# Tile-wise waits between pools, and another order of loads at the head of a channel loop, in a kernel for attention and state-space gradients

## The chip, the core and the metric

The kernel runs on one core of a Trainium2 chip. The metric is the time of one execution on the device in microseconds (us), as a median over runs. Engines are named as in the profile: PE (matmuls), PEld (its weight loads), DVE (VectorE), ACT (ScalarE), POOL (GpSimd) and SP (SyncE, here only a queue that issues DMAs).

## What is computed

The reference is the forward value and the gradients, with respect to twelve inputs, of a gate between two branches:

```python
g = sigmoid((x * gate_w).sum(-1))
a = attention(x, wqkv, wo)                       # S=2048, D=576, 32 heads of 18
b = ssm_conv(x, A, B, C, log_dt, Dskip)          # 576 channels, 128 complex states each
out = g * a + (1 - g) * b
grads = vjp(out)(grad_out)                       # x, wqkv, wo, A, B, C (re, im), log_dt, Dskip, gate_w
```

The convolution's kernel is a sum over states of powers of a complex number per channel; the program computes it by blocks of 128 positions, with a scan over the 16 blocks that carries the state.

## The kernel before

The program is written in four stages, one after the other, each with its own memory pools, opened at its start and closed at its end.

*First stage* (lines 116 to 335). Loads x, the weights and grad_out, transposes, projects Q, K and V, which it stores to QKV_d in DRAM, computes grad_out times wo transposed (dO, lines 245 to 266: ten matmuls for each half of a tile, an evacuation by VectorE or ScalarE, a store to dO_d on SP's queue) and the parameters of the states (lines 268 to 335, stores to par_d). The order on each engine is found by the framework's scheduler, from its own model of time.

*Attention* (lines 429 to 827). Forward and backward in one software pipeline of 1024 steps plus a tail: a step G makes two score products and an exp for the forward pass (PT, line 799) and, OFF = 39 steps later, the backward products, an exp (eb, line 804) and two elementwise products on VectorE (ds, line 809). PT tiles are kept from the one to the other in a pool of 41 buffers of 2 KB per partition (ptp). In the last 39 of the steps with backward work no PT is made. Blocks of ds are transposed by DMA, some by PE (turn, lines 553 to 565), and VectorE copies the transposed ones from PSUM. Meanwhile POOL builds the table of powers E_d for the next stage (lines 343 to 427). The order on all engines, SP included, is that of the source (manual_schedule, line 436). The last work is the gradient stores dqkv_d, issued by POOL (line 537).

*Channel loop* (lines 828 to 1183). The 576 channels are taken in 18 blocks of 32. For each block the program loads windows of x and of the weighted gradient (m_load: xs, gyp), two halves of E (load_en: E1n), parameters (load_par) and, for each pair of blocks, RXn (load_rx); m_part makes correlations (psM), copied to mst by ScalarE and stored to Md_d; m_skw reads them back skewed from DRAM, m_sum and m_fin reduce them into two columns of RX; prep_rx makes the other columns of RX (three ScalarE instructions on RXn); turn_e transposes E with PE and copies it from PSUM; uv projects RX on E (UV); scan runs along the 15 block steps on VectorE (lines 984 to 999: one copy, line 989, then three operations a step); casts, rw1, rw2, t0, ybp, pairs1, pairs2 and sums turn that into outputs and gradient sums; k0 and t0_load take the convolution's first taps through Kp_d in DRAM to T0w. The order on PE, ScalarE, VectorE and POOL is that of the source (line 873); SP's queue is ordered by the scheduler. The lead-in, lines 1112 to 1133, prepares block 0 and part of block 1; the loop then runs from i = -1, where each pass works on block i and prepares i+1, i+2 and i+3. Three pools hold its tiles in SBUF: s4c (results), s4l (constants and gyp) and s4lw (all else).

*Last stage* (lines 1185 to 1393). Loads x, grad_out, the gradient of Q, K and V (dq_all, in four pieces) and others, computes the gradient of wqkv (ps_dwq, line 1257), finishes the states' gradients on VectorE (pool pf), stores them through transposes (emit_dn), closes that pool and opens another in its place (pbwork, line 1329) for the loop over the 16 tiles of tokens (ps_a, ps_dx), which transposes dq_all by DMA (dqT, line 1348).

A pool that opens on the bytes of closed pools waits, all its tiles together, until every user of those pools is done.

Of the kernel before, what the change touches and what calls it, by code (L numbers as in the profile page):

```python
# [17 lines left out]
P = 128  # L18


def build(tc, aps, dbg_aps=None, stages=("s1", "attn", "post", "s4", "final")):
# [40 lines left out]
    with ExitStack() as gctx:  # L62
# [366 lines left out]
        if "attn" in stages:  # L429
# [4 lines left out]
            NFILL = {"V": 1, "Q": 0, "K": 0}  # L434
            with ExitStack() as ctx:
                ctx.enter_context(tc.manual_schedule(engines={mybir.EngineType.PE, mybir.EngineType.Activation, mybir.EngineType.DVE, mybir.EngineType.Pool, mybir.EngineType.SP}))
                ga = ctx.enter_context(tc.tile_pool(name="ga", bufs=2))
                ptp = ctx.enter_context(tc.tile_pool(name="ptp", bufs=41))
                work = ctx.enter_context(tc.tile_pool(name="awork", bufs=2))
                apsp = ctx.enter_context(tc.tile_pool(name="aps", bufs=1, space=bass.MemoryType.PSUM))  # L440
                ident_f = work.tile([P, P], F32, tag="ident_f", bufs=1, name="ident_f")
                nc.vector.tensor_copy(ident_f, ident_bf)

# [109 lines left out]
                def turn(tiles, outs):  # L553

                    pt_ = apsp.tile([P, len(tiles), TPQ, P], BF, tag="accB", name="turn_p")
                    for x, t_ in enumerate(tiles):
                        for qb in range(TPQ):
                            nc.tensor.transpose(pt_[:, x, qb, :], t_[:, qb * P:(qb + 1) * P], ident_bf)  # L558

                    def ev():  # L560
                        x = 0
                        for n, o_ in outs:
                            nc.vector.tensor_copy(o_(), pt_[:, x:x + n])  # L563
                            x += n
                    return ev

# [261 lines left out]
        if "s4" in stages:  # L828
            XB = 2 * CB
            GS = 16  # L830

            s4c_cm = tc.tile_pool(name="s4c", bufs=1)
            s4c = s4c_cm.__enter__()
            SS = s4c.tile([P, 6, D], F32, name="SS")
            CK = s4c.tile([P, 2, 2, D], BF, name="CK")
# [2 lines left out]
            nc.vector.memset(ones_f, 1.0)  # L838

            with ExitStack() as ctx:  # L840
                pc = ctx.enter_context(tc.tile_pool(name="s4l", bufs=1))
                pw = ctx.enter_context(tc.tile_pool(name="s4lw", bufs=1))
                pps = ctx.enter_context(tc.tile_pool(name="s4lps", bufs=1, space=bass.MemoryType.PSUM))
                pidx_i = pc.tile([P, 1], mybir.dt.int32, name="pidx_i")
                nc.gpsimd.iota(pidx_i, pattern=[[0, 1]], base=0, channel_multiplier=1)
                l0col = pc.tile([P, 1], F32, name="l0col")
# [8 lines left out]
                                        base=SUB - 1, pattern=[[SUB, NSUB]], channel_multiplier=-1)  # L855
                gyp2 = []
                for u in range(2):
                    g_u = pc.tile([P, 2 * SUB, CB], BF, name=f"gyp{u}")
                    nc.vector.memset(g_u[:, SUB:2 * SUB, :], 0.0)
                    gyp2.append(g_u)  # L860
                mst2 = []
# [14 lines left out]
                RXs, BK = {}, {}  # L876
                ydx = {}

                def load_rx(xb):
                    d0 = xb * XB  # L880
                    RXn = pw.tile([P, 2 * NB, XB], BF, tag="RXn", bufs=1, name="RXn")
                    nc.sync.dma_start(RXn[:, 0:NB, :], xr_d[:, :, d0:d0 + XB])
                    nc.sync.dma_start(RXn[:, NB:2 * NB, :], gyr_d[:, :, d0:d0 + XB])
                    RXs[xb] = [RXn, None]

                def prep_rx(xb):
# [5 lines left out]

                xss = {}

                def m_load(b):
                    xs = xss[b] = pw.tile([P, NSUB, SUB, CB], BF, tag="xs", bufs=2, name="xs")
                    src = bass.AP(tensor=xb_d.tensor, offset=xb_d[b:b + 1, 0:1, 0:1].offset,
                                  ap=[[XR * SUB * CB, NB], [SUB * CB, NSUB], [1, NSUB * SUB * CB]])
                    nc.sync.dma_start(xs.rearrange("p e t c -> p (e t c)"), src)
                    nc.sync.dma_start(gyp2[b % 2][:, 0:SUB, :].rearrange("p t c -> p (t c)"), gyb_d[b])  # L900

                def m_part(b, u):
                    d0 = b * CB
# [39 lines left out]
                        B_ = BK[b] = dict(E={}, En={})  # L943
                    return BK[b]

                def turn_e(b, h, q0, q1):

                    B_ = blk(b)
                    if q0 == 0:
                        B_["E"][h] = pw.tile([P, GS, 2, N], BF, tag="E1e", bufs=2, name="E1e")  # L950
                    En, E_ = B_["En"][h], B_["E"][h]
                    for q in range(q0, q1):
                        pt_ = pps.tile([P, 4, 2, N], BF, tag="bk", bufs=4, name="etp")
                        for c_ in range(4):
                            for ri in range(2):
                                nc.tensor.transpose(pt_[:, c_, ri, :], En[:, 4 * q + c_, ri, :], ident_bf)  # L956
                        nc.scalar.copy(E_[:, 4 * q:4 * q + 4], pt_)  # L957

                def load_par(b):
                    par = blk(b)["par"] = pw.tile([P, 12, CB], F32, tag="par", bufs=2, name="par")  # L960
                    nc.sync.dma_start(par, par_d[:, 0:12, b * CB:(b + 1) * CB])

                def load_en(b, h):
                    dG = b * CB + h * GS
                    En = blk(b)["En"][h] = pw.tile([P, GS, 2, P], BF, tag="E1n", bufs=6, name="E1n")
                    nc.sync.dma_start(En, E_d[:, dG:dG + GS])

                def uv(b, h):
                    B_ = blk(b)
# [139 lines left out]
                    src = bass.AP(tensor=Kp_d.tensor, offset=Kp_d[b:b + 1, 1:2, 0:1].offset, ap=[[CB, P], [1, P * CB]])  # L1109
                    nc.sync.dma_start(T0w.rearrange("p j c -> p (j c)"), src)  # L1110

                m_load(0)
                load_rx(0)
                load_en(0, 0)
                load_par(0)
                load_en(0, 1)
                m_load(1)
                m_part(0, 0)
                m_part(0, 1)
                m_skw(0)  # L1120
                turn_e(0, 0, 0, 2)
                prep_rx(0)
                turn_e(0, 0, 2, 4)
                m_sum(0)
                m_fin(0)
                k0(0)
                t0_load(0)
                load_en(1, 0)
                load_en(1, 1)
                load_en(2, 0)  # L1130
                load_en(2, 1)
                m_part(1, 0)
                m_part(1, 1)
                for i in range(-1, NBLK):
                    cur = i >= 0
                    nx = i + 1 < NBLK
                    mb = i + 3 if i + 3 < NBLK else None
                    sb = i + 2 if i + 2 < NBLK else None
                    if sb is not None:
                        m_skw(sb)  # L1140
                    if sb is not None:
                        load_par(sb)
                    if mb is not None:
                        m_load(mb)
                    if sb is not None and sb % 2 == 0:
                        load_rx(sb // 2)
                    if nx and cur:
                        k0(i + 1)
                    if nx:
                        uv(i + 1, 0)  # L1150
                        turn_e(i + 1, 1, 0, 4)
                    if sb is not None and sb % 2 == 0:
                        prep_rx(sb // 2)
                    if cur:
                        scan(i, 0, 15)
                        casts(i)
                        rw1(i)
                        rw2(i)
                        t0(i, 0)
                        t0(i, 1)  # L1160
                    if nx:
                        uv(i + 1, 1)
                    if cur:
                        if nx:
                            t0_load(i + 1)
                        ybp(i, 0)
                        ybp(i, 1)
                        pairs1(i)
                    if cur and mb is not None:
                        load_en(mb, 0)  # L1170
                        load_en(mb, 1)
                    if sb is not None:
                        turn_e(sb, 0, 0, 4)
                        m_sum(sb)
                        m_fin(sb)
                    if cur:
                        pairs2(i)
                        sums(i)
                    if mb is not None:
                        m_part(mb, 0)  # L1180
                        m_part(mb, 1)
                    if cur:
                        BK.pop(i)

        if "final" in stages and "s4" in stages:
# [12 lines left out]
                eng.tensor_tensor(out, a, b, op=op)  # L1198

            with ExitStack() as ctx:  # L1200
                pb = ctx.enter_context(tc.tile_pool(name="pb", bufs=1))
                pps = ctx.enter_context(tc.tile_pool(name="pps", bufs=2, space=bass.MemoryType.PSUM))
                pbw = ctx.enter_context(tc.tile_pool(name="pbw", bufs=2))
                x_tok = pb.tile([P, NT, D], BF, name="x_tok_b")
                nc.sync.dma_start(x_tok, x_v)
                dq_all = pb.tile([P, NT, FPAD], BF, name="dq_all")
# [9 lines left out]
                tt(ggo, g_t, omg_t, A.mult)  # L1216

                with ExitStack() as actx:
                    pf = actx.enter_context(tc.tile_pool(name="pf", bufs=1))
                    pfw = actx.enter_context(tc.tile_pool(name="pfw", bufs=2))  # L1220

                    def load_dq(u):
                        f0, fn, c0 = FQS[u]
# [102 lines left out]
                    nc.vector.tensor_copy(rowb2, dDs_row)  # L1326
                    nc.gpsimd.dma_start(aps_out["out_11"].rearrange("(o d) -> o d", o=1), rowb2)

                work = ctx.enter_context(tc.tile_pool(name="pbwork", bufs=2))
                sgo = pb.tile([P, NT], F32, name="sgo")  # L1330
                dsg = pb.tile([P, NT], F32, name="dsg")
                dsgb = pb.tile([P, NT], BF, name="dsgb")
# [107 lines left out]
```

## Time and profile before

| | |
|---|---|
| median of 3 runs | 2973.82 us (2972.2 to 2982.99) |
| the profiled execution | 2978.26 us, its span 2976.5 us |
| busy in the span | PE 2468.2 us (83%), ACT 2373.2 (80%), DVE 2359.4 (79%), POOL 1605.9 (54%) |
| mean granted TensorE clock | 0.917 |
| first exp of attention | 206.13 us |
| last exp of attention, end | 2179.22 us |
| last attention matmul on PE, end | 2187.06 us |
| first scan of the channel loop | 2239.15 us |
| first ps_dwq matmul of the last stage | 2782.41 us |
| first dqT matmul of the token loop | 2869.47 us |

Times of single instructions are microseconds from the span's start. In a timeline a row holds start, duration, engine, line, operation, output and inputs with sizes, count, and in brackets how long the engine had been idle and what ended that. SPq and ACTq are DMA issues on the queues of SP and ScalarE: their duration is the time in which the issuing engine was held, not that of the transfer. The chain of waits is followed back from the last instruction; a row "DMA a<-b" in it is the wait from the issue of a transfer until its data has landed.

### The profile page before, as it was taken

What the parts mean: (1) busy time and instruction counts of PE and PEld (TensorE: products, weight loads), DVE (VectorE), ACT (ScalarE), POOL (GpSimd) and SP (SyncE); (2) the same over time, 40 slices, a digit from 0 to 9 for tenths busy, and PEclk for the clock granted to TensorE, in tenths of its full rate; (3) what the DMA queues carried; (4) which work ended last, traced back from release to release, by engine and by line L of the source; (5) the groups of instructions that cost most, each with busy time, mean ns of one, the idle gap of its engine ahead of it and who ended that gap; (6) DMA issues with size and microseconds to landing.
All of it is one profiled execution on the core that took longest, in us unless ns stands there. A gap on an engine that the chain in (4) does not pass through costs nothing.

```text
span 2976.5 us, 69573 instructions
## 1 busy us (share of the span) xinstructions
PE 2468.2 (83%) x27132; PEld 1186.9 (40%) x27132; DVE 2359.4 (79%) x4147; ACT 2373.2 (80%) x2765; POOL 1605.9 (54%) x2653
## 2 busy tenths in 40 slices
PE   4768988998988888889898889898847887876779
PEld 2432333332333233233333233333226777776457
DVE  4435998997998889799899889989937888889634
ACT  2449999999999999899999999999736777675111
POOL 1038888888887788778888878878010000000010
PEclk8877999998999999899999999999968888887889
DMA  8855999989989989998988998998788877872886
GB/s 224 160 152 107 159 155 169 163 158 165 171 147 165 167 155 167 160 157 155 168 165 154 164 161 153 166 165 153 130 196 217 209 201 208 206 194 66 244 211 132
DMA packets 1293343, 499.99 MB, mean 168 GB/s; under 512 B 1187774, under 2 KB 1263136, under 8 KB 1283796
## 3 DMA queue, kind: packets, MB, share of 16 engines
q1 hardware_dynamic: 1264500, 434.91, 77.2%
q0 software_dynamic: 20624, 53.26, 7.3%
q10 hardware_dynamic: 7888, 7.38, 0.8%
q8 instruction: 212, 3.47, 0.5%
q14 instruction: 119, 0.97, 0.1%
HBM read 144.48 MB, written 99.69 MB: 82 GB/s over the span
## 4 chain that ended last, share of the span: by engine, by line
ACT 34%; DVE 23%; PE 21%; DMA 8%; issue 7%; POOL 4%; SPq 3%; ACTq 0%; DVEq 0%; POOLq 0%
ACT eb L804 20%; ACT PT L799 13%; PE ps_P L30 7%; DVE ds L809 7%; DVE tz L995 3%; DVE HG L999 2%; DVE tz L998 2%; PE accV L30 2%; DMA gT<-gb 2%; PE turn_p L558 2%; PE ps_dx L30 2%; DVE pq L1065 2%; PE ps_dwq L30 1%; POOL et L358 1%; PE accK L30 1%
## 5 line engine op out<-in xcount | busy, mean ns | idle before, releaser
L809 DVE TENSOR_TENSOR ds<-ps_P,PT 128x512 bf16<-128x512 f32 x2048 | 1312.0, 683 | 123.0 <-PE ps_P L30 83.8
L804 ACT ACTIVATE eb<-ps_P 128x1024 bf16<-128x1024 f32 x1024 | 1098.6, 1073 | 71.9 <-PE ps_P L30 70.7
L799 ACT ACTIVATE PT<-ps_P 128x1024 bf16<-128x1024 f32 x1024 | 1101.8, 1078 | 3.7 <-PE ps_P L30 2.5
L30 PE MATMUL ps_P<-dOaT,VaT_g 32*128 32x512 bf16 x2048 | 581.4, 390 | 32.8 <-DVE ds L809 18.3
L358 POOL TENSOR_TENSOR et<-eG,eT 128x448 f32<-128x448 f32 x576 | 542.0, 961 | 10.7
L30 PE MATMUL ps_P<-QaT_g,KaT_g 32*128 32x512 bf16 x2048 | 416.3, 398 | 143.9 <-ACT PT L799 128.5
L30 PE MATMUL ps_P<-KaT_g,QaT_g 32*128 32x512 bf16 x2048 | 408.5, 391 | 2.2 <-ACT eb L804 1.6
L30 PEld LDWEIGHTS <-KaT_g 32*128 32x128 bf16 x2048 | 148.2, 92 | 477.4 <-issue 462.0
L358 POOL TENSOR_TENSOR Eo<-et,et 128x448 bf16<-128x448 f32 x288 | 327.0, 1135 | 20.8
L1101 POOL TENSOR_TENSOR SS<-m 128x96 f32<-128x96 f32 x18 | 7.9, 441 | 556.9 <-ACT m L1099 556.9
L30 PEld LDWEIGHTS <-QaT_g 32*128 32x128 bf16 x2048 | 116.1, 91 | 286.4 <-issue 264.7
L30 PE MATMUL accO<-PT,Vtok_g 128*32 128x512 bf16 x2048 | 214.4, 405 | 0.0
L30 PE MATMUL accV<-eb,dOa 128*32 128x512 bf16 x2048 | 185.3, 395 | 27.6 <-ACT eb L804 27.4
L30 PE MATMUL accK<-dsT,Qtok_g 128*32 128x256 bf16 x4096 | 166.2, 285 | 4.5 <-DMA dsT<-ds 2.8
L558 PE MATMUL turn_p<-ident_bf,ds 128*128 128x128 bf16 x1664 | 137.3, 227 | 29.9 <-DVE gb L630 28.8
L30 PE MATMUL accQ<-ds,Ktok_g 128*32 128x512 bf16 x2048 | 159.2, 388 | 3.2 <-DVE gb L612 2.6
L957 ACT COPY E1e<-etp 128x1024 bf16<-128x1024 bf16 x144 | 135.9, 1044 | 20.0 <-PE etp L956 14.6
L563 DVE COPY dsT<-turn_p 128x1024 bf16<-128x1024 bf16 (+1 forms) x224 | 144.2, 644 | 4.9 <-PE turn_p L558 4.9
L30 PEld LDWEIGHTS <-Vtok_g 128*32 128x32 bf16 x2048 | 53.8, 93 | 225.4 <-issue 224.6
L30 PE MATMUL yp<-Rw,E1n 128*128 128x30 bf16 x1152 | 67.8, 232 | 83.5 <-DVE Rw L1020 69.0
L30 PEld LDWEIGHTS <-E1n 128*128 128x128 bf16 x2304 | 96.5, 108 | 101.0 <-issue 100.5
L558 PEld LDWEIGHTS <-ds 128*128 128x128 bf16 x1664 | 100.5, 101 | 78.6 <-issue 78.6
(247 smaller groups left out, 3704.2 us busy)
## 6 DMA issues: line engine op xcount, KB each, us to landing
E_d<-Eo POOLq DMA_DIRECT2D x144, 256.0 KB, 3.8
E1n<-E_d SPq DMA_DIRECT2D x36, 1024.0 KB
xs<-xb_d SPq DMA_DIRECT2D x18, 1024.0 KB
T0w<-Kp_d SPq DMA_DIRECT2D x18, 1024.0 KB
Md_d<-mst SPq DMA_DIRECT2D x36, 288.0 KB
dsT<-ds SPq DMA_TRANSPOSE x512
dqkv_d<-dtk POOLq DMA_DIRECT2D x96, 72.0 KB, 4.4
QKV_d<-stg SPq DMA_DIRECT2D x12, 504.0 KB
```

The costliest lines, as they stand in the source:

```text
L30: return nc.tensor.matmul(out, lhsT=lhsT, rhs=rhs, start=start, stop=stop, **kw)
L358: nc.gpsimd.tensor_tensor(out, a, b, op=op)
L558: nc.tensor.transpose(pt_[:, x, qb, :], t_[:, qb * P:(qb + 1) * P], ident_bf)
L563: nc.vector.tensor_copy(o_(), pt_[:, x:x + n])
L799: nc.scalar.activation(U["PT"][i, j // 2], ps, ACT.Exp)
L804: nc.scalar.activation(e, ps, ACT.Exp)
L809: nc.vector.tensor_tensor(U["ds"][i][:, j, :], ps, U["PT"][i, j // 2][:, j % 2, :], op=A.mult)
L957: nc.scalar.copy(E_[:, 4 * q:4 * q + 4], pt_)
L995: nc.vector.tensor_tensor(tz, HG[:, :, k - 1, :].unsqueeze(1).to_broadcast([P, 2, 4, CB]), ZZ, op=A.mult)
L998: nc.vector.tensor_tensor(t0v, t0v, UVk[:, :, :, k, :], op=A.add)
L999: nc.vector.tensor_tensor(HG[:, :, k, :].rearrange("p (r s) c -> p r s c", s=2), t0v, t1v[:, ::-1], op=A.add)
L1065: nc.vector.tensor_tensor(o.rearrange("p a b n c -> p a b (n c)"), a_.rearrange("p b n c -> p b (n c)").unsqueeze(1).to_broadcast([P, 2, 2 ...
```

## The change

All pools of attention, of the channel loop and of the last stage are opened with reuse_waits="tile": a tile of such a pool waits only for the users of those earlier tiles that lay on its own bytes (in PSUM, on its own bank). The channel loop's loaded tiles (gyp, xs, RXn, par, E1n) go into a pool of their own, s4ld, between s4l and s4lw. The lead-in is written anew: block 0's loads are issued by ScalarE, in the order xs, RXn, gyp, E1n, par; inside the lead-in SP's queue too follows the source; two transposed halves of E are copied by VectorE instead of ScalarE; what was the loop's pass i = -1 is part of it; and in pass i = 0 prep_rx(1) stands behind t0 instead of ahead of the scan. In attention's tail, from the last forward step on and for OFF steps, the copies of transposed tiles are made by ScalarE.

```diff
-                ga = ctx.enter_context(tc.tile_pool(name="ga", bufs=2))
+                ga = ctx.enter_context(tc.tile_pool(name="ga", reuse_waits="tile", bufs=2))
...
-                            nc.vector.tensor_copy(o_(), pt_[:, x:x + n])
+                            (nc.scalar.copy if NTOT <= now[0] < NTOT + OFF else nc.vector.tensor_copy)(o_(), pt_[:, x:x + n])
...
+                pl_ = ctx.enter_context(tc.tile_pool(name="s4ld", reuse_waits="tile", bufs=1))
...
-                def load_rx(xb):
+                def load_rx(xb, dma=nc.sync.dma_start):
...
-                    RXn = pw.tile([P, 2 * NB, XB], BF, tag="RXn", bufs=1, name="RXn")
+                    RXn = pl_.tile([P, 2 * NB, XB], BF, tag="RXn", bufs=1, name="RXn")
...
-                m_load(0)
-                load_rx(0)
-                load_en(0, 0)
-                load_par(0)
-                load_en(0, 1)
-                m_load(1)
-                m_part(0, 0)
-                m_part(0, 1)
-                m_skw(0)
-                turn_e(0, 0, 0, 2)
-                prep_rx(0)
-                turn_e(0, 0, 2, 4)
-                m_sum(0)
-                m_fin(0)
-                k0(0)
-                t0_load(0)
-                load_en(1, 0)
-                load_en(1, 1)
-                load_en(2, 0)
-                load_en(2, 1)
-                m_part(1, 0)
-                m_part(1, 1)
-                for i in range(-1, NBLK):
-                    cur = i >= 0
+                dve_copy = nc.vector.tensor_copy
+                act_dma = nc.scalar.dma_start
+                with tc.manual_schedule(engines={mybir.EngineType.SP}):
+                    m_load(0, act_dma, lambda: load_rx(0, act_dma))
+                    load_en(0, 0, act_dma)
+                    load_par(0, act_dma)
+                    m_part(0, 0)
+                    m_part(0, 1)
+                    m_skw(0)
+                    load_en(0, 1)
+                    prep_rx(0)
+                    turn_e(0, 0, 0, 4, dve_copy)
+                    m_sum(0)
+                    m_fin(0)
+                    m_load(1)
+                    uv(0, 0)
+                    load_en(1, 0)
+                    turn_e(0, 1, 0, 4, dve_copy)
+                    uv(0, 1)
+                    k0(0)
+                    load_par(1)
+                    m_part(1, 0)
+                    m_part(1, 1)
+                    t0_load(0)
+                    m_skw(1)
+                    load_en(1, 1)
+                    m_load(2)
+                    turn_e(1, 0, 0, 4)
+                    m_sum(1)
+                    m_fin(1)
+                    m_part(2, 0)
+                    m_part(2, 1)
+                    load_en(2, 0)
+                    load_en(2, 1)
+                for i in range(NBLK):
+                    cur = True
...
-                    if sb is not None and sb % 2 == 0:
+                    if sb is not None and sb % 2 == 0 and i > 0:
                         prep_rx(sb // 2)
...
+                    if i == 0:
+                        prep_rx(1)
...
-                pb = ctx.enter_context(tc.tile_pool(name="pb", bufs=1))
+                pb = ctx.enter_context(tc.tile_pool(name="pb", reuse_waits="tile", bufs=1))
...
-                work = ctx.enter_context(tc.tile_pool(name="pbwork", bufs=2))
+                work = ctx.enter_context(tc.tile_pool(name="pbwork", reuse_waits="tile", bufs=2))
```

## The prediction

> **What bounds the kernel now.** I read the page's chain by line first (exps and ds products of attention, then the scan's tz and HG), then the chain in order of time around each change of stage, since only there can the diff act. The chain between attention and the channel loop (start us, us, what):
>
> ```profile
> 2196.55 0.58 SPq L899 DMA_DIRECT2D xs<-xb_d  x1
> 2197.18 0.59 SPq L882 DMA_DIRECT2D RXn<-xr_d  x1
> 2197.82 5.43 SPq L883 DMA_DIRECT2D RXn<-gyr_d  x1
> ...
> 2207.95 2.94 SPq L913 DMA_DIRECT2D Md_d<-mst  x2
> ```
>
> ```profile
> 2193.38 2.87 DMA dqkv_d<-dtk
> ...
> 2207.95 12.58 DMA Md_d<-mst
> ...
> 2221.25 2.79 DMA skw<-Md_d
> ```
>
> The first (timeline of SP's queue) shows that no load of the loop starts until the last gradient store of attention has landed at 2196.25, though PE's last attention matmul ended at 2187.06. The second (the chain) shows a store of 12.58 us: the Md_d pair queued with E1n, E1n and xs, 3 MB issued in the 5 us before it. When the loop runs steadily the same pair lands in 3.5 us (issued by 2282.94, its reader issues at 2286.46). VectorE's timeline has the scans' first copies:
>
> ```profile
> 2239.15 0.23 DVE L989 CAST HG<-UV 128x128 f32<-128x128 bf16 x1 [50.57 <-ACT UV L982]
> ...
> 2275.06 0.22 DVE L989 CAST HG<-UV 128x128 f32<-128x128 bf16 x1
> ...
> 2302.09 0.22 DVE L989 CAST HG<-UV 128x128 f32<-128x128 bf16 x1
> ```
>
> From block 1 on, blocks follow at 27.0 and 31.1 in turn (block 3 starts at 2333.14) and VectorE sets the pace (50.6 busy of 58). So what counts is the time of block 1's scan, 2275.06: any gain there is kept. Three other seams have the same shape, a pool's release that a load waits for (chain):
>
> ```profile
> 2762.20 5.27 DMA yd_d<-yd
> ...
> 2768.05 14.31 DMA dq_all<-dqkv_d
> ...
> 2864.03 5.39 DMA dqT<-dq_all
> ```
>
> (the second pool is released by the dlrowb store that lands at 2859.5) and the timeline at attention's start:
>
> ```profile
> 191.42 0.44 SPq L289 DMA_DIRECT2D par_d<-t  x1
> 193.75 2.37 SPq L460 DMA_DIRECT2D KaT_g<-QKV_d  x4
> ...
> 204.84 1.28 ACT L799 ACT_TABLE_LOAD   x1 [13.81 <-DMA Vtok_g<-QKV_d]
> ```
>
> The profiled execution took 2978.26 us (span 2976.5), 4.4 above the median 2973.82. Gains are differences within the span; I take their sum off the median.
>
> **Part by part.** By "tile", a new tile waits only for the users of the tiles that lay on its own bytes.
>
> *Attention's start.* Its operand tiles lie at the front, over x_pad and wqkv_sb, whose last readers are the projections near 158; only the stores to QKV_d (last issued 158.57) are then needed. Loads can slide under the 160 dO matmuls, which end at 190.56. Earliest first exp: 190.56 + 0.6 for two products + 1.28 table load = 192.4 against 206.13, so 13.7. But the loads (2.4 + 1.5 + 0.6 + 5.0 of SP's time) are moved past the dO_d stores on SP's queue, and PE's two halves already wait for those (11 us of waits by both copying engines). I give back 4.7: **9**. Ends −3 (stores of dO_d late by a load each time, no load early enough) and 14.
>
> *Tail copies.* From the last PT exp (2111.5) to the last eb exp (2179.2) VectorE is busy 9.3 to 10 of 10 us, ScalarE about 6. Some 10 copies of 0.644 (L563's mean) leave VectorE: 6.4 at most. On ScalarE the nearest row is E1e<-etp, same shape, 1.04; two per eight steps raise it to about 7.6 of 10, but they are queued ahead of that step's exp, which accV and the next ps_P wait for. Ends −2 (exps late by the copies) and 6; **3**, because ScalarE has the room.
>
> *Lead-in.* The tiles of the loads get a pool of their own, which by the sizes lies from about 27 to 102 KB, over the 41 PT buffers (24 to 106 KB). PT's low buffers have their last reader tens of microseconds before the end. ScalarE issues xs, RXn twice, gyp, E1n and par: by SP's rows 0.58+0.59+5.43+0.5+1.48+0.43 = 9.0 us of issue, at the latest behind the last exp at 2179.2; queued behind it are only the mst copies (wanted at 2188). xs took 7.5 from issue to first matmul, so psM can start when PE leaves attention, 2187.1. Then: psM 2.1, copy 0.6 (2189.9); Md_d store 0.9 + 3.5 as in the steady loop (2194.2); skw and its sums 5.2, as at 2220.54 to 2225.73 (2199.5); m_fin 0.5; uv of half 0 3.2 (2203.2); transposes of half 1 copied by VectorE at 0.69 (L563's shape; VectorE is idle here) and uv, together 4.3: scan 0 at 2207.5 instead of 2239.15, 31.6 earlier. prep_rx(0), 7.6 on ScalarE, runs beside the store and skw (2190 to 2197.6), hidden; without that cover it would cost its 7.6.
>
> What is late next is block 1. Its m_part follows at 2210, store and skw again 9.6: 2220.5. SP in source order issues xs(2) only behind T0w, those skw and E1n: 2218.7 + 7.5 = 2226.2. Queued behind m_part(2) on PE and ScalarE: k0(1), uv(1,0), turn_e(1,1), casts(0): 3.3+2.2+3.2+3.8+2.1 gives 2240.8. prep_rx(1) now comes after casts(0), so hR no longer waits for it (9.3 us before pq), but uv(1,1) does: 7.6 + 2.1. Scan 1: 2250.5, so **25** are kept. If m_part(0) slips among attention's last PE work, from 2179.2 to 2187 half idle, and xs(2) lands 5 sooner, it is up to 40; if the store and skw keep their old lengths (8 more), 15.
>
> Here a rule weighs against the change. The Trainium skill, DMA: Bandwidth & Descriptors, section Issuing engines are not separate DMA queues, says that transfers started by different engines share the same 16 engines and interleave, so that another issuer saves issue time alone. By it the store would still take 12.58 and the gain be 25 − 8 = 17. The row says why it took that: 3 MB in flight. The diff also puts E1n(0,1) and xs(1) behind skw, so they aren't in flight; that comes of the order and not of the queue. I take the row.
>
> *Opening of the last stage.* x_tok lies over constants, gyp and xs, free after block 17's k0 (2717); dq_all reaches over the E1n buffers, whose last reader ends at 2761.55. So dq_all starts 6.0 sooner (the yd_d landing and SP's waits go), and x_tok, 2.36 MB at the 375 GB/s of 2770 to 2790, no longer stands ahead of it: 6.3. **12**; ends 5 (x_tok not early) and 14.
>
> *The token loop's pool.* PE finished ps_dwq at 2846 and met dqT at 2869.47. OT and y_b lie on zz and Wri, whose readers end near 2827; dqT lies on opad, read until 2848 to 2853. With issue and landing 5.4: 2853.5 to 2858.3, 11 to 16 earlier. **11**, since later dqT waits (7.05 at 2893.93, 7.31 at 2913.55) show those transposes near their limit; low end 4.
>
> memsets, ggo and the per-tile waits: nothing seen to cost; they lie on POOL and DVE idle at the seams, and cost under 2 us bare.
>
> Sum 9 + 3 + 25 + 12 + 11 = 60: 2973.8 − 60 = **2914**. Low ends −3−2+15+5+4 = 19: 2955. The last three have no end below nothing: their loads can only come before the release that held them. High ends 14+6+40+14+17 = 91: 2883.
>
> **Rivals.** (A) Only the lead-in moves: elsewhere the order that the scheduler writes into SP's queue keeps loads behind the old stores. 25 + 3: 2946. For: SP's queue is in order; against: loads were issued within 0.1 us of the release, so the release held them. (B) The lead-in gets its best case: m_part(0) inside attention's tail, 15 more: 2899 (with the starts at their high ends, 2885). Speaks for it: PE busy 4.7 of 7 us there; against: its PSUM banks are held by the last scores. (C) The rule is right and bytes still overlap late tiles: 8.5 us of issue remain, 2965. (D) Slower: loads of the last stage enter SP's queue inside the channel loop and wait at its head for a slot; E1n, xs and par stand behind. One block then waits once per such load; a 3.6 us slip per block over 17 blocks eats the 60, and from there on it is slower; at 5 per block 2999. Against: only k0(17)'s tiles free so late, with few loads behind.
>
> **How the numbers follow.** Forecast 0.50, A 0.22, B 0.17, C 0.06, D 0.05. Half a per cent, about what this measurement can tell, is 15 us. Forecast, A and B are faster by more: 0.89; C within: 0.06; D: 0.05. The range 2883 to 2955 takes A and most of B in and leaves C, D and a little more out.
>
> **What would show it.** First exp near 197; xs issued by ScalarE's queue at or before 2180; Md_d's store about 4 us; scan 0 near 2195 and scan 1 near 2238 in the new trace (the 12 from before it included), then 27 and 31 as before; first ps_dwq about 8 after the last yp; dqT about 10 after the last ps_dwq. It is wrong if block periods grow, if attention's middle lengthens by loads in its tail, or if the gain at scan 1 is under 15.

## The result and the profile after

The changed kernel took 2957.08 us (median of 4 runs, 2954.24 to 2960.32), the kernel before 2973.01 on the same chip (4 runs, 2971.79 to 2982.99): ratio 0.9939, 95% interval 0.9915 to 0.9964. That is 15.9 us faster where 60 had been forecast, and just above the range's upper end of 2955. The profiled execution after took 2954.24 us, its span is 2952.5 us.

The span is 24.0 us shorter than before, 8 more than the medians differ: the profiled execution before lies 5 above its kernel's median, the one after 3 below. I cut both spans at the same milestones; a column of differences says where the 24 came from:

| stretch | before | after | gain | forecast |
|---|---|---|---|---|
| start to first exp | 206.13 | 202.85 | 3.3 | 9 |
| first exp to last PT exp | 1904.3 | 1895.3 | 9.0 | 0 |
| last PT exp to last eb exp (the tail) | 67.8 | 77.7 | -9.9 | 3 |
| last eb exp to scan 1 | 96.9 | 83.9 | 13.0 | 25 |
| scan 1 to the last block's scan | 460.4 | 460.1 | 0.3 | 0 |
| last scan to first ps_dwq | 47.0 | 44.5 | 2.5 | 12 |
| first ps_dwq to first dqT product | 87.1 | 77.6 | 9.5 | 11 |
| first dqT product to the end | 107.0 | 110.7 | -3.7 | 0 |

The 9.0 in attention's middle can't be put to the change. In the eleven kernels of this document with tile-wise waits in attention that stretch took 1895.3 to 1912.5 us (mean 1901.4), in the three without 1901.4 to 1904.3 (mean 1903.2); a difference of a us or two isn't excluded. Without it the profile's gain is 15.0.

Attention's start, timeline of SP's queue and then of ScalarE:

```profile
191.36 0.45 SPq L289 DMA_DIRECT2D par_d<-t  x1
191.87 2.60 SPq L460 DMA_DIRECT2D KaT_g<-QKV_d  x4
...
197.29 0.58 SPq L471 DMA_DIRECT2D QaT_g<-QKV_d  x1
```

```profile
190.98 1.28 ACT L799 ACT_TABLE_LOAD   x1
202.85 4.81 ACT L799 ACTIVATE PT<-ps_P 128x1024 bf16<-128x1024 f32 x5 [10.58 <-PE ps_P L30]
```

ScalarE's table load ahead of the first exp moves up from 204.84 to 190.98 (it waits for nothing any more), while the loads move only from 193.75 to 191.87: KaT still starts 0.06 us after the last par_d store has been issued. It is no longer the landing of that store that holds them, but their place behind it in the queue.

The tail, by slices of ten microseconds; the columns are slice, length, busy time of PE, PEld, DVE, ACT and POOL with their instructions, granted clock, DMA share and GB/s. First before, then after:

```profile
2110.00:2120.00 10.00, 7.90 (x94) 2.46 (x92) 9.78 (x19) 6.80 (x8) 1.36 (x2) 1.00 0.77 145
2120.00:2130.00 10.00, 7.29 (x72) 2.52 (x72) 9.32 (x18) 5.91 (x6) 0.00 (x0) 1.00 0.63 120
```

```profile
2110.00:2120.00 10.00, 9.04 (x61) 2.11 (x60) 7.28 (x13) 5.94 (x7) 0.00 (x0) 0.53 0.62 119
2120.00:2130.00 10.00, 9.04 (x78) 2.90 (x77) 6.89 (x12) 6.12 (x7) 1.23 (x2) 0.50 0.52 100
```

VectorE did fall from 9.3 to 9.8 of ten to about 7, as reckoned, but PE took its place: at half the granted clock it is busy 9 of 10 and does less (362 matmuls in the five slices from 2110, against 446). The clock's fall to 0.5 is at 2110.6; it lasts to 2192.5.

The lead-in. First the issues on ScalarE's queue, then PE's last attention matmuls (accK) and its first of the loop, before and after:

```profile
2176.22 0.62 ACTq L900 DMA_DIRECT2D xs<-xb_d  x1
2176.88 0.60 ACTq L883 DMA_DIRECT2D RXn<-xr_d  x1
2177.52 5.93 ACTq L884 DMA_DIRECT2D RXn<-gyr_d  x1
2183.70 2.88 ACTq L902 DMA_DIRECT2D gyp<-gyb_d  x1
```

```profile
2185.16 1.90 PE L30 MATMUL accK<-dsT,Qtok_g 128*32 128x256 bf16 x32 [0.78 <-DVE dsT L563]
```

```profile
2186.15 1.04 PE L30 MATMUL accK<-dsT,Qtok_g 128*32 128x256 bf16 x16 [2.23 <-DMA dsT<-ds]
2189.94 2.16 PE L30 MATMUL psM<-xs,gyp 128*32 128x128 bf16 x32 [2.75 <-DMA gyp<-gyb_d]
```

The loads do start 20 us earlier. But attention's last matmuls on PE now wait 2.23 us for a transpose by DMA, so that PE leaves attention 11.3 us after the last exp's start (8.9 before), and block 0's first product (psM) waits another 2.75 us for gyp, which ScalarE could issue only at 2183.70.

The store of block 0's Md_d and its reader on SP's queue:

```profile
2191.81 1.32 SPq L915 DMA_DIRECT2D Md_d<-mst  x2
2197.19 2.56 SPq L928 DMA_DIRECT2D skw<-Md_d  x4
```

Then the chain of waits between scan 0 and scan 1, first before, then after, and VectorE's first copies of each block's scan after:

```profile
2242.06 7.53 DMA gyp<-gyb_d
...
2258.24 4.02 DMA RXn<-gyr_d
```

```profile
2214.97 4.20 DMA Md_d<-mst
...
2222.96 12.24 DMA gyp<-gyb_d
...
2243.73 6.23 DMA RXn<-gyr_d
...
2250.06 4.07 ACT RX L890
```

```profile
2211.28 0.23 DVE L991 CAST HG<-UV 128x128 f32<-128x128 bf16 x1 [1.61 <-ACT UV L984]
2259.71 0.23 DVE L991 CAST HG<-UV 128x128 f32<-128x128 bf16 x1 [6.49 <-ACT UV L984]
2286.63 0.22 DVE L991 CAST HG<-UV 128x128 f32<-128x128 bf16 x1
2317.68 0.22 DVE L991 CAST HG<-UV 128x128 f32<-128x128 bf16 x1
```

Block 0's store of Md_d is read 4.4 us after its second half's issue at 2192.77 (12.58 before), block 1's after 4.20. Scan 0 is 27.9 earlier, and then nearly half of that is gone: scan 1 follows 48.4 us later (35.9 before). The same two transfers stand between them as before, and both are longer: block 2's gyp takes 12.24 us (7.53), RXn(1) 6.23 (4.02). From scan 1 on the periods are 27 and 31 as before.

The opening of the last stage, SP's queue, and the token loop's start, VectorE:

```profile
2746.58 0.54 SPq L1064 DMA_DIRECT2D yd_d<-yd  x1
2747.23 3.38 SPq L1221 DMA_DIRECT2D x_tok_b<-in_A_x_dram  x1
2750.70 8.60 SPq L1240 DMA_DIRECT2D dq_all<-dqkv_d  x2
```

```profile
2841.83 0.76 DVE L1373 TENSOR_TENSOR dif<-ps_a,y_b 128x576 f32<-128x576 f32 x1 [1.59 <-PE ps_a L30]
2847.90 0.82 DVE L1375 SCALAR_TENSOR_TENSOR o0b<-dif,g_t,y_b 128x576 bf16<-128x576 f32 x1 [5.31 <-DMA out_dram<-dlrowb]
```

x_tok is issued 0.65 us after the yd_d store, dq_all right behind x_tok: again the queue's order. In the token loop dqT's wait is gone, and a new one is there: o0b, the first output tile, waits 5.31 us for the dlrowb store.

### The profile page after: what moved, and what is told of

Read it like the earlier page. It is cut to its first block, busy times and chain, and to the rows that moved or that the text cites. A ratio compares the mean times of both kernels' runs of the same rounds, so it can differ in the third digit from the quotient of the medians.

```text
span 2952.5 us, 69590 instructions
## 1 busy us (share of the span) xinstructions
PE 2484.4 (84%) x27132; PEld 1192.8 (40%) x27132; DVE 2358.0 (80%) x4146; ACT 2371.7 (80%) x2766; POOL 1610.5 (55%) x2653
## 5 line engine op out<-in xcount | busy, mean ns | idle before, releaser
L809 DVE TENSOR_TENSOR ds<-ps_P,PT 128x512 bf16<-128x512 f32 x2048 | 1311.1, 682 | 130.6 <-PE ps_P L30 87.4
L959 ACT COPY E1e<-etp 128x1024 bf16<-128x1024 bf16 x136 | 128.2, 1039 | 17.0 <-PE etp L958 17.0
L30 PEld LDWEIGHTS <-E1n 128*128 128x128 bf16 x2304 | 96.5, 108 | 90.6 <-issue 90.1
L558 PEld LDWEIGHTS <-ds 128*128 128x128 bf16 x1664 | 101.5, 101 | 73.3 <-issue 73.3
```

Of the source, the lines that this page charges most:

```text
L30: return nc.tensor.matmul(out, lhsT=lhsT, rhs=rhs, start=start, stop=stop, **kw)
L809: nc.vector.tensor_tensor(U["ds"][i][:, j, :], ps, U["PT"][i, j // 2][:, j % 2, :], op=A.mult)
```

## The experiments

Each ratio is to the kernel before on the same chip in the same batch (medians 2979.9, 2981.1 and 2978.7 us for the three batches), with its 95% interval. These intervals are 0.003 to 0.005 wide, some 8 to 15 us, so I judge a stage by its own stretch in the profile and the whole by the ratio. The stretches in us:

| kernel | first exp | tail | last eb to scan 1 | last eb to scan 3 | last scan to ps_dwq | ps_dwq to dqT | dqT to end | ratio |
|---|---|---|---|---|---|---|---|---|
| before | 206.1 | 67.8 | 96.9 | 154.9 | 47.0 | 87.1 | 107.0 | 1 |
| after | 202.9 | 77.7 | 83.9 | 141.8 | 44.5 | 77.6 | 110.7 | 0.9939 |
| e1_tail_dve | 204.3 | 68.6 | 87.4 | 145.3 | 44.6 | 79.4 | 110.6 | 0.9928 |
| e2_tail_act_only | 205.9 | 73.3 | 99.5 | 157.7 | 46.5 | 86.1 | 107.0 | 1.0014 |
| e3_tile_only | 202.8 | 66.3 | 88.7 | 146.7 | 44.8 | 78.1 | 111.6 | 0.9927 |
| e4_lead_only | 206.5 | 67.9 | 86.0 | 143.2 | 46.8 | 86.8 | 107.5 | 0.9970 |
| e5_open_pool | 204.6 | 66.2 | 90.1 | 147.2 | 36.6 | 89.9 | 111.9 | 0.9945 |
| e6_start_pool | 193.1 | 72.5 | 92.0 | 150.0 | 45.0 | 77.6 | 112.2 | 0.9901 |
| e7_block1 | 200.4 | 69.2 | 79.4 | 143.3 | 45.0 | 77.3 | 112.4 | 0.9911 |
| e8_all | 190.1 | 66.6 | 80.3 | 144.1 | 36.6 | 88.8 | 110.8 | 0.9874 |
| e9_block1_skw | 202.2 | 68.2 | 78.0 | 142.9 | 44.6 | 77.9 | 112.0 | 0.9906 |
| e10_open_bufs | 204.8 | 76.5 | 93.1 | 150.6 | 36.6 | 76.7 | 112.4 | 0.9932 |
| e11_best | 192.6 | 66.1 | 75.8 | 136.8 | 36.5 | 76.9 | 111.3 | 0.9827 |
| e12_best_act | 193.2 | 76.2 | 75.8 | 136.5 | 36.6 | 76.7 | 111.7 | 0.9852 |

**The parts of the change, apart.** First the changed kernel with the tail copies back on VectorE:

```diff
-(nc.scalar.copy if NTOT <= now[0] < NTOT + OFF else nc.vector.tensor_copy)(o_(), pt_[:, x:x + n])
+nc.vector.tensor_copy(o_(), pt_[:, x:x + n])
```

> The changed kernel with attention's tail copies back on VectorE. Theory 1 (ScalarE's copies are what drops the granted TensorE clock to 0.50 in the tail): the tail from the last PT exp to the last eb exp goes back from 78 to 68 us, its clock to about 1.0 until the last 10 us, and the whole to some 2947, 10 below the changed kernel's 2957. Rival (the clock drop is a matter of chance or phase and the copies gain what was forecast): 2957 to 2960, and the clock in the tail is low in some profiles of either version.

Measured: 2960.57 us, ratio 0.9928 (0.9906 to 0.9950). The clock is 1.0 in most of the tail again and the tail takes 68.6, as theory 1 has it, but the median gains only some 3 us on the changed kernel's ratio, within the uncertainty and nearer to the rival. The reverse, that line alone in the kernel before:

> The kernel before with only the tail copies given to ScalarE. Theory 1: tail clock 0.50 from the first copy on, tail 78 us, the whole 2983, 10 above before. Rival (chance): near 2970 to 2973, clock as before. The forecast on record was 3 below before.

Measured: 2984.55 us, ratio 1.0014 (1.0000 to 1.0029): 4 us slower. The clock falls to 0.5 at 2137.5, 19 us after the first moved copy and not with it as theory 1 had it, and stays there; the tail takes 73.3.

Next, the word "tile" on all pools and nothing else of the change:

```diff
-tc.tile_pool(name="ga", bufs=2)
+tc.tile_pool(name="ga", reuse_waits="tile", bufs=2)
...
-tc.tile_pool(name="pbwork", bufs=2)
+tc.tile_pool(name="pbwork", reuse_waits="tile", bufs=2)
```

> The kernel before with tile-wise waits in all its pools and nothing else. Theory 2 (the order of SP's queue keeps loads behind the old stores at attention's start and at the opening of the last stage, so only the landing of one store is saved at each; the token loop's pool gives its 6 to 10): 3 + 3 + 6 to 10, plus up to 9 in the lead-in for the landing of the last gradient stores: 2952 to 2961. Rival (tile-wise waits are worth what was forecast, 9 + 12 + 11 and some lead-in): 2935.

Measured: 2959.33 us, ratio 0.9927 (0.9905 to 0.9950). Within the uncertainty, all that the change gives is had by this alone. By the table: 3.3 at the start, 8.2 at scan 1, 2.2 at the opening, 9.0 before dqT, less 4.5 after it, 18.2 in sum; the ratio makes it 22. And the lead-in alone (the lead-in and the channel loop's pools as changed, attention's and the last stage's pools and the tail as before):

> The changed kernel with the lead-in alone: the channel loop's pools tile-wise and its lead-in as changed, the tail copies on VectorE, attention's and the last stage's pools as before. By the changed kernel's trace the lead-in brings scan 1 13 us nearer to attention's last exp with a tail at half clock; Theory 3 (block 1's loads, 4 MB issued within 8 us, set scan 1): 13 to 15 below before, 2958 to 2960. Rival (the half clock at the tail's end spoiled the lead-in as well): the forecast 25, 2948.

Measured: 2970.82 us, ratio 0.9970 (0.9956 to 0.9984): 9 us, less than the 13 to 15 that were expected. Scan 1 comes 10.9 sooner after attention than before. Four kernels have tile-wise waits with the old lead-in (e3, e5, e6, e10) and need 88.7 to 93.1 us to scan 1; three have the change's lead-in (after, e1, e4) and need 83.9 to 87.4. So the waits give 4 to 8 us and the new order of loads, which the forecast had as its largest part, 1 to 9, some 5 in the mean; to scan 3 it is the same (146.7 to 150.6 against 141.8 to 145.3).

**Do the loads stand behind others in SP's queue?** To the kernel with tile-wise waits alone, x_tok and the first piece of dq_all are moved to GpSimd's queue, ahead of its memsets, and the last block's two sums (eng) to VectorE:

```diff
-nc.sync.dma_start(x_tok, x_v)
+nc.gpsimd.dma_start(x_tok, x_v)
...
-load_dq(0)
+nc.gpsimd.dma_start(dq_all[:, :, c0:c0 + fn], dqkv_d[:, :, f0:f0 + fn])
...
+eng = nc.vector if b == NBLK - 1 else nc.gpsimd
```

> Tile-wise waits alone in the stages before it, and the last stage's x_tok and its first quarter of dq_all issued by GpSimd's queue instead of SP's, where they had stood behind the last yd_d store and behind each other; the last block's two sums go from GpSimd to VectorE, so that nothing in GpSimd's stream stands ahead of the loads. Theory 2 (only the order of SP's queue keeps these loads late): x_tok is issued some 20 us ahead of the last yp, dq_all when the E1n buffers fall free; from the first copy of scan 1 to the first ps_dwq 494 to 498 us in place of the 504.6 of the kernel with tile-wise waits alone; total 2949 to 2953 (that kernel: 2959.3). Rival (the landing itself, 13 to 14 us with so much in flight, sets ps_dwq, or what is gained is lost to the next quarter of dq_all): 501 to 505, total 2957 to 2961.

Measured: 2963.48 us, ratio 0.9945 (0.9925 to 0.9964). The stage did what theory 2 said: x_tok is issued at 2727.33, 17 us ahead of the last yp, and from scan 1 to ps_dwq 495.1 us pass (504.6 in e3; 8.3 of the gain lie behind the last scan). The total missed what both sides expected, since the stretch after it grew by 11.8. ScalarE's timeline shows by what:

```profile
2774.89 0.51 ACT L1262 CAST dwq_bf<-ps_dwq 128x426 bf16<-128x426 f32 x1 [0.47 <-DMA out_dram<-dwq_bf]
2786.40 0.34 ACTq L1263 DMA_DIRECT2D out_dram<-dwq_bf  x1
2786.83 0.51 ACT L1262 CAST dwq_bf<-ps_dwq 64x426 bf16<-64x426 f32 x1 [11.43 <-DMA dq_all<-dqkv_d]
```

The cast was done at 2775.4; the issue of its store came 11 us later, after a wait that the profile puts down to a load of dq_all, the next cast stood behind it in ScalarE's stream, and PE behind the casts.

The same for attention's start: QaT(0) and the four KaT pieces on GpSimd's queue, ahead of its two memsets of dOa:

```diff
-nc.sync.dma_start(t_, strip("K", g, m * KB, KB))
+(nc.gpsimd if g == 0 else nc.sync).dma_start(t_, strip("K", g, m * KB, KB))
...
+load_piece("QaT", 0, 0)
 load_full(0)
+for dOa_u in dOa2: nc.gpsimd.memset(dOa_u, 0.0)
```

> Tile-wise waits alone, and attention's first QaT and four KaT loads issued by GpSimd's queue, which has nothing to do from 8 us to 181 us, ahead of its two dOa memsets. Theory 2 (these loads came late because they stand behind the dO_d and par_d stores in SP's queue, not because their bytes were held): first exp at 192 to 195 instead of 202.8; total 2950 to 2953. Rival (the next thing is late instead, the Vtok transposes that still stand in SP's queue, or the bytes are held until the dO products end): first exp at 199 or later, or an exp row broken by waits for accO, total 2957 to 2961.

Measured: 2953.20 us, ratio 0.9901 (0.9878 to 0.9925). GpSimd's timeline, then ScalarE's:

```profile
182.83 0.73 POOL L470 DMA_DIRECT2D QaT_g<-QKV_d  x1 [0.63 <-issue]
183.56 2.75 POOL L459 DMA_DIRECT2D KaT_g<-QKV_d  x4
```

```profile
191.77 1.28 ACT L803 ACT_TABLE_LOAD   x1
193.06 3.77 ACT L803 ACTIVATE PT<-ps_P 128x1024 bf16<-128x1024 f32 x4
```

The first exp is at 193.06, 9.7 sooner, and starts as the table load ends: the order of the queue had held it till 202.8. This profile, with VectorE's copies, has a clock of 0.5 from 2100 to 2138.

**What holds scan 1.** Changed kernel, VectorE's copies, and another lead-in: E1n(1,1) and RXn(1) are loaded earlier, block 1's uv comes before m_part(2), which moves into pass 0 behind t0(0), with prep_rx(1) after it:

```diff
+load_en(1, 1)
 m_part(1, 0); m_part(1, 1)
+load_rx(1)
 t0_load(0); m_skw(1)
 m_load(2)
 turn_e(1, 0, 0, 4); m_sum(1); m_fin(1)
-m_part(2, 0); m_part(2, 1)
+uv(1, 0); turn_e(1, 1, 0, 4); uv(1, 1)
```

> The changed kernel with VectorE's tail copies (2960.6), and its lead-in put in another order: block 1's E1n and RXn(1) are loaded ahead of the wait for block 1's Md_d store, uv of block 1 stands ahead of m_part(2) on PE and ScalarE, and prep_rx(1) comes after block 0's casts. Theory 3 (scan 1 waits for block 2's xs and gyp, and for RXn(1) behind skw(2), because they stand ahead of it in PE's and ScalarE's streams): scan 1 follows scan 0 after 27 to 30 us instead of 50.1, total 2938 to 2943. Rival (bytes are the limit from attention's end to scan 1: 16 queues' worth of loads have to land whatever their order, or block 2 is late instead): scan 1 gains under 6, or scan 2 gives it back; total 2954 to 2960.

Measured: 2955.20 us, ratio 0.9911 (0.9891 to 0.9930). Scan 1 follows scan 0 after 39.0 us (50.1 without the edit), a gain of half the size that was expected; and scan 3 follows scan 2 after 36.2 instead of 31. The total is the rival's. SP's queue, and PE at the reader of skw:

```profile
2220.84 0.92 SPq L915 DMA_DIRECT2D Md_d<-mst  x2
...
2222.88 4.90 SPq L884 DMA_DIRECT2D RXn<-gyr_d  x1
...
2229.31 2.60 SPq L928 DMA_DIRECT2D skw<-Md_d  x4
```

```profile
2234.45 0.60 PE L30 MATMUL misc<-sel,skw 128*128 128x8 f32 x2 [12.32 <-DMA skw<-Md_d]
```

RXn's issue, held for 4.90 us, stood ahead of skw. All three edits together:

> All three at once on the changed kernel with VectorE's tail copies: the new order of the lead-in, attention's first loads and the last stage's first loads on GpSimd's queue. If the three theories hold the gains add, since each lies in a stage of its own: 2960.6 - 20 - 9 - 9 = 2922, between 2917 and 2930. If the rivals hold: 2945 to 2960.

Measured: 2942.80 us, ratio 0.9874 (0.9853 to 0.9896). That lies just below the rivals' 2945: start and opening gain 10 to 14 and 8 us, but the loss after ps_dwq (88.8) and at scan 3 come with them.

**Mending what those showed.** In the lead-in, RXn(1) behind skw, RXn(2) one block earlier:

```diff
-load_rx(1)
 t0_load(0); m_skw(1)
+load_rx(1)
...
+if i == 1: load_rx(2)
```

> The kernel with block 1's part in a new order, with RXn(1) loaded behind skw(1) instead of ahead of it, and RXn(2) loaded one block earlier. Theory 3, amended (there scan 1 still came 39.0 us after scan 0 because the gyr_d load held SP's queue 4.9 us ahead of skw(1), which was read at 2237, 13 us after its store had been issued): skw(1) is read some 5 to 8 us sooner, scan 1 follows scan 0 after 30 to 34 us, and scan 3 follows scan 2 after 31 instead of 36; total 2943 to 2948 (that kernel: 2955.2). Rival (the bytes: E1n(1,1), Md_d and skw share the engines, so the wait only changes its name): scan 1 after 37 to 40, total 2952 to 2956.

Measured: 2948.24 us, ratio 0.9906 (0.9888 to 0.9923). Scan 1 after 35.1, scan 3 after 29.8 us, but scan 2 now after 35.1 instead of 27.7: to scan 3 it is the same (142.9 and 143.3), and so is the ratio. Scan 1 lies between theory and rival; that the wait only changes its name, as the rival said, holds of scan 3. In the last stage, the dwq_bf stores by GpSimd, out of six buffers:

```diff
-ob = pbw.tile([P, FQ], BF, tag="dwq_bf", name="dwq_bf")
+ob = pfw.tile([P, FQ], BF, tag="dwq_bf", bufs=6, name="dwq_bf")
-nc.scalar.dma_start(out_dwqkv[...], ob[...])
+nc.gpsimd.dma_start(out_dwqkv[...], ob[...])
```

> The kernel with the last stage's first loads on GpSimd's queue, and the stores of dwq_bf on GpSimd's queue too, with six buffers for dwq_bf instead of two. In that kernel the first ps_dwq came 8.3 us sooner, but 11.8 us were lost before the first dqT product: ScalarE stood 11.4 us at the issue of a dwq_bf store, until a load of dq_all had landed. Theory 4 (the gain was lost to ScalarE's stores, whose issue waits for older transfers and holds its casts, and with them the two banks of ps_dwq): the stretch from the first ps_dwq to the first dqT product falls from 89.9 to 75 to 80 us, total 2945 to 2950 (that kernel: 2963.5; tile-wise waits alone: 2959.3). Rival (bytes: the second half of dq_all, wo and wqkv are no sooner there, so PE waits for them): 85 to 90, total 2958 to 2963.

Measured: 2955.68 us, ratio 0.9932 (0.9909 to 0.9954), above what was expected, since the whole shows no gain over tile-wise waits alone. The stretch itself fell to 76.7 as expected; PE's timeline has all 320 ps_dwq matmuls in one piece:

```profile
2782.54 62.20 PE L30 MATMUL ps_dwq<-dq_all,x_tok_b 128*128 128x426 bf16 x320 [5.95 <-DMA dq_all<-dqkv_d]
```

The profiled execution lost its gain elsewhere: 1912.5 us in attention's middle and 76.5 in the tail, with the clock at 0.5. But at 2973.32 us it is the slowest of six (the others 2949 to 2956), so it doesn't explain the median. A gain of 8 us is near the uncertainty of the ratio; why it doesn't show is open. All of it together:

> All of it together: the changed kernel with VectorE's tail copies, the lead-in's new order with skw(1) ahead of RXn(1), attention's first loads, the last stage's first loads and the dwq_bf stores on GpSimd's queue. If the two theories of this batch hold: 2942.8 - 9 - 11 = 2923, between 2917 and 2930. If both rivals hold: 2938 to 2943.

Measured: 2925.11 us (2924.75 to 2928.92, 4 runs), ratio 0.9827 (0.9812 to 0.9842), in the range that was expected if both theories hold. It is the best of these kernels, 1.1 points below the change. VectorE's scans:

```profile
2201.07 0.23 DVE L995 CAST HG<-UV 128x128 f32<-128x128 bf16 x1 [1.70 <-ACT UV L988]
2235.75 0.22 DVE L995 CAST HG<-UV 128x128 f32<-128x128 bf16 x1
2267.06 0.22 DVE L995 CAST HG<-UV 128x128 f32<-128x128 bf16 x1
2296.74 0.22 DVE L995 CAST HG<-UV 128x128 f32<-128x128 bf16 x1
```

And that kernel with the change's tail copies on ScalarE:

> The kernel with all of it together, with attention's tail copies on ScalarE as in the change. Theory 1 (with the copies on ScalarE PE's granted clock falls to 0.5 at the tail's start and stays there to attention's end, because PE then works in shorter pieces; six profiles with VectorE's copies show at most a dip that recovers): clock 0.5 to 0.6 through most of the tail, 73 to 78 us from the last PT exp to the last eb exp, median 3 to 8 above the kernel with all of it together. Rival (the dip at the change of stage falls by chance, one profile with VectorE's copies had 0.5 for 30 us too): clock 1.0 through the tail, about 64 to 67 us, median equal within 2 or lower.

Measured: 2930.03 us, ratio 0.9852 (0.9828 to 0.9876), 5 to 7 us slower than with VectorE's. The tail's slices:

```profile
2120.00:2130.00 10.00, 9.40 (x84) 2.91 (x80) 7.92 (x13) 6.25 (x7) 1.17 (x2) 0.50 0.90 132
2130.00:2140.00 10.00, 8.84 (x61) 2.23 (x61) 7.17 (x13) 5.82 (x6) 1.18 (x2) 0.50 0.57 109
```

## Why the prediction was wrong, step by step

The direction was right. Every gain of the sum came out smaller, by the table of stretches: the tail by 12.9 us, the lead-in by 12.0, the opening by 9.5, the start by 5.7, the token loop by 5.2 with what it gave back.

**Lead-in, 25: measured 13.0.** Two steps failed. The first is "psM can start when PE leaves attention, 2187.1": it took attention's end as fixed and block 0's loads as landed by then, and put at nothing what 20 us earlier loads do to attention's own transfers. PE left attention 2.5 us later after the last exp (the 2.23 for the transpose), and psM waited 2.75 more for gyp, since ScalarE's six issues took 11.9 us and not the 9.0 of the sum. It is no accident of one profile: in all eight kernels whose block 0 loads stand in ScalarE's queue, PE leaves attention 11.3 to 16.2 us after the last exp's start, and psM waits another 2.3 to 2.8 for gyp; in the six others PE leaves after 6.9 to 8.9. That cost 5.2 us.

The second is "xs(2) ... 2218.7 + 7.5 = 2226.2". Block 2's window was issued at 2222.37, 0.8 later than the first step explains, and its product psM began at 2235.24, 12.9 us after the issue in place of 7.5: 5.4 us. Its last part is the gyp row, 12.24 us against 7.53 for the same load in the old lead-in. The 16 DMA engines were full in both waits (shares of 1.02 and 0.98, where a transfer counts at its start), but moved 3.2 MB in the one and 1.7 MB in the other. So other loads stood in it. This is where the rule of the Trainium skill that transfers share the engines, whoever issues them (DMA: Bandwidth & Descriptors, section Issuing engines are not separate DMA queues), did weigh. I had set it aside because the new order took bytes away from the Md_d store. That was right of the store and wrong of the stage. 5.2 + 0.8 + 5.4 make the 11.4 of the 11.6 us by which scan 1 is late against the forecast, both counted from the last exp; the rest of the sum held: 14.7 from psM to prep_rx(1) (14.6), 9.7 from there to scan 1 (9.7). RXn(1), though on the chain, cost nothing: ScalarE finished its casts at 2249.92 and RXn had landed at 2249.96. The cover that I had named held too: prep_rx(0) cost nothing.

Rival C, given 0.06, named the mechanism, late tiles behind overlapping bytes. That bytes are the limit up to scan 3 isn't shown. The DMA engines' share is 1.02, 0.93, 0.93 and 0.89 in the four 20 us slices from 2180 after the change, and 0.52, 1.12, 0.94 and 0.88 in the kernel before: the change filled the first slice alone. Six kernels with three orders of a new lead-in (after, e1 and e4; e7 and e8; e9) need 142 to 145 us to scan 3, which fits a limit by bytes; but e11, with e9's lead-in, needs 136.8 and e12 136.5, and why is not settled. One reading of the lines was off without weight in the sum: a load of the loop, gyp, was issued at 2189.80 already, ahead of the last gradient store's landing.

**Opening of the last stage, 12: 2.5. Attention's start, 9: 3.3.** One step failed in both: I read from loads "issued within 0.1 us of the release" that the release alone held them, and let them slide under earlier work. They also stood behind the old stores in SP's queue, and an order of issue doesn't show while a later wait covers it. Rival A (0.22) named this. It was tested by leaving the waits and moving the loads to another queue (in e5 with two sums moved off that queue's engine): 8.3 us at the opening (e5), 9.7 at the start (e6). With that the first exp is at 193.06, where I had 192.4 as the earliest. So the sizes that I had worked out for bytes that fall free early were about right, and the claim that SP's queue would use it was wrong. In the last stage it needed a second edit (e10) to be kept.

**Tail copies, 3: a loss of 3 to 7.** The step "because ScalarE has the room" looked at ScalarE and VectorE and took PE's speed as given. In all three profiles with ScalarE's copies the clock falls to 0.5 before the tail's middle and stays there to attention's end, but for 3.4 us in e12 (tails of 73.3 to 77.7 us); of eleven with VectorE's copies nine have tails of 66 to 69, and two (e6, e10) a long fall too (72.5, 76.5). So the fall happens without them, and with them each time. The medians agree: the copies cost 1.4 thousandths (e2), 1.1 (after against e1) and 2.5 (e12 against e11), each near its uncertainty. So do the mean clocks of all executions on record: 0.911 (12 executions of e2) against 0.914 (23 before), 0.914 (4) against 0.919 (6), 0.919 (5) against 0.926 (4). What pulls the clock down is open. The Trainium skill (TensorE: Matmul & The Clock Gate, section What's actually happening) ties the half clock to an idle window of about 3.4 us; in the 12 us ahead of the fall at 2110.6 PE was never idle for more than 0.83 us. It ran the same instructions there, with gaps within 0.1 us of those where the clock stayed at 1.0 (e3); the first moved copy started only 1.6 us before the fall. By that rule the clock should have stayed up; the measurement decides.

**Token loop, 11: 9.5, less 3.7 that were given back.** The size and the cause of the gain were right. The end of the sum was not: "later dqT waits" proved no limit, but o0b's wait for the dlrowb store (5.31 us) was new, and it stands on the chain that ended last. All kernels with "tile" in this stage show 110.6 to 112.4 after the first dqT product, those without it 107.0 to 107.5. That this one wait makes the whole difference was not tested.

**Channel loop, no change: right.** Periods of 27 and 31, 460.1 us; rival D (loads at the head of SP's queue) didn't occur.

Of the milestones I named, ScalarE's issue before 2180 (2176.22), the store near 4 us and the periods came true. Scan 0, forecast near 2195, came at 2211.28, and scan 1, near 2238, at 2259.71; both forecasts held 12 us of gains in attention, of which 2.4 were left at the last exp. I had written that the forecast is wrong if the gain at scan 1 is under 15: after attention's last exp it is 13.0.

## What to carry to other kernels

A finer release only permits a transfer to start earlier; whether it does is decided by what stands ahead of it in its queue, which the trace doesn't show as long as the coarse wait ends later. So read the queue's own order at the seam, and move the load to a queue that is empty there, before taking the gain into a sum (here 18 us at two seams). Where the DMA engines are already full (here shares of 0.9 and more), a chain of latencies taken from a quieter stretch overstates what a new order brings: look at what else moves beside each transfer, and count among the losers the transfers of the stage that is still ending.

## What was not expected of the hardware

PE's granted clock can halve while PE has had no idle stretch over 0.83 us in the 12 us before, and stay there for over 60 us with PE busy 9 of 10 (0.53 and 0.50 above). It depends on the execution, and it went with what another engine does (three of three profiles against two of eleven).

An issue of a transfer can hold the issuing engine for long: 5.93 us for RXn<-gyr_d on ScalarE's queue, 4.90 for it on SP's. In e5 a store of dwq_bf stood 11 us before its issue, and ScalarE's casts behind it stood still in that time.
